# A fused attention and mixer kernel: each side piece gets a place of its own in TensorE's list

## The chip, the core and the metric

The kernel runs on one core of a Trainium2 chip. A core has five engines, each with its own list of instructions that it works through strictly in order: TensorE (PE: matrix products and transposes, with the loads of their stationary operand shown as PEld), VectorE (DVE), ScalarE (ACT), GpSimd (POOL) and SyncE (SP), which here issues all DMA transfers. Engines wait for one another by semaphores. The metric is the device time of one execution in microseconds (us); lower is better. 1% of it, about 6.3 us, is about what a measurement of this kernel can tell from no change.

## The reference, cut to what matters

Four batches (called blocks 0 to 3), 8 heads, 576 positions, head dimension 64, model dimension 512. All weights come as float32 in the low and high words of 64-bit integers and are put together on the chip.

```python
# attention of one batch: a low-resolution softmax attention (means over 4 positions)
s = scale * np.matmul(qq, kk.transpose(0, 1, 3, 2))            # 144 x 144
a = softmax(s);  out_up = np.repeat(np.matmul(a, vv), 4, axis=2)
# plus a local one, |i - j| < 4
scores = np.where(mask, scale * np.matmul(q, k^T), -1e9);  out_local = np.matmul(softmax(scores), v)
# gated convolution: 5 taps along the sequence
gate = 1.0 / (1.0 + np.exp(-gate_pre));  x = (gate * (x @ w_val)) @ w_out
# mixer: over the tokens, then over the channels
h = np.maximum(xt @ w_tok1, 0.0) @ w_tok2;   u = x + h.transpose(0, 2, 1)
h2 = np.maximum(u @ w_ch1, 0.0) @ w_ch2;     return u + h2
```

## The kernel before

**Products.** Every float32 product is split in three: operands are cut into a high and a low part (`hi_lo`, L707), and `mm3` (L273) issues high·high, high·low, low·high. A product row of the trace therefore shows lines L275, L276, L277 in turn. Most have 288 moving columns, half a block's sequence.

**Stages.** `start()` is attention of block 0 in an order written out by hand. Then `first_products` (L889) runs the main stream, per block b: `p1(b)` (L728) with the products p_val (gate times value; y = p_val * gate on VectorE, L747), p_x (output projection, into u_sb), transposes, r_ps (first token product; r_hl on VectorE, L812) and p_h (second token product; u_sb = p_h + u_sb on VectorE, L826, then split to u_hl by ScalarE and GpSimd, L708/L709); then `c1(b)` (L836), the first channel product g_ps in 24 items of 12 matmuls (12 weight tiles f, two sequence halves; 1.6 us each). 12 of the 24 items are issued right after p1(b); the other 12 go between the pieces of p1(b+1) as FILL says (L50). In block 3 all 24 follow at once.

**The second channel product** is done by a scheme with 7 products instead of 8 (two halves of d_ff by two halves of the sequence). It needs, for each of the 6 pairs of weight tiles, four relu results and four sums of them. `c1` makes them: ScalarE writes a relu result into r_sb after each item (L876), after each second weight tile VectorE makes 4 sums of 128x288 (L883), and all 7 slots go to DRAM in `r_dr` (L884). `c2` (L904) loads the slots back (r_back), splits them (g_hl) and multiplies them with ch2 weights (p_o). It runs from 490.24 to 624.41 us of the span. Its last piece adds p_o of two row halves m = 0, 1 into u_back (L927) and stores them (L934).

**Side pieces.** While the main stream runs, `mix` (L990) drops in pieces of other generators: attention of blocks 1 to 3 (`attention(b)`, L329: 26 steps each, four head pairs with low scores sc_d, local scores sc_l, softmax, turns pt_d and pt_l, outputs o_d and o_l into x_f; after each head pair the 5 taps of the convolution, L446 and L449, on VectorE), decoding of the token weights (`w_t1`, `w_t2`), of the ch2 weights (`ch2_new`), and the first two loads of `c2`. Each has a start and an end in microseconds of matmul work of the main stream (T_AT, A_AT, W2_AT, C2_AT), and its steps are spread evenly between. In block 0's c1, the channel weights are decoded too, tile by tile (`ch1_new`: L144, L146, L149, L160 on VectorE, four instructions per 128x256 chunk).

**What sets the order.** TensorE executes in the order in which the program is written. The other four lists are made by a scheduler from dependencies, priorities and its own costs, so moving a piece on TensorE moves rows on all of them. sc_d and sc_l share two PSUM banks: a sc_l product may start only when ScalarE has read (exp, L322) the sc_d that stands in its bank, and the exps wait for VectorE's maxima (mx, L316).

## Time and profile before

| | |
|---|---|
| median of 3 runs | 633.72 us (632.38 to 636.26) |
| profiled execution, whole | 631.51 us |
| its span, first to last instruction | 629.7 us |
| mean granted TensorE clock | 0.963 of full |
| TensorE busy | 585.0 us (93% of the span) |
| VectorE busy | 450.5 us (72%) |
| ScalarE busy | 338.9 us (54%) |
| GpSimd busy | 143.3 us (23%) |

A row of a timeline gives start, duration, engine, line, operation, output<-inputs, shapes, count, and in square brackets how long the engine was idle before it and what released it. A row of a table of windows gives for each engine its busy time and number of instructions, then the granted TensorE clock (1.00 is 2.4 GHz, 0.50 is 1.2 GHz), the share of DMA time used and GB/s. L numbers are lines of the kernel.

### The profile page before, as it was taken

Reading aid. Unit: us, or ns where it says so; the run is one execution under the profiler, and the core shown is the slowest. Engines: PE = TensorE matmul, PEld = TensorE weight load, DVE = VectorE, ACT = ScalarE, POOL = GpSimd, SP = SyncE. Lnnn points to the kernel's source line nnn. Section 1 sums busy time; section 2 is a strip of 40 time slices with the busy share of each in tenths; the row PEclk is TensorE's granted clock in tenths of the full one; section 3 lists DMA queues with packets and bytes.
Section 4 is the critical chain, followed back from the end, with each engine's and each line's share of the span. In section 5 each row is a group of like instructions: output and inputs, shape, how many; then the busy total and the mean of one; then the engine's idle time right before and its main releaser. Section 6 shows DMA issues by size and latency. Waiting matters only on the chain.

```text
span 629.7 us, 13126 instructions
## 1 busy us (share of the span) xinstructions
PE 585.0 (93%) x4975; PEld 536.6 (85%) x4975; DVE 450.5 (72%) x967; ACT 338.9 (54%) x1118; POOL 143.3 (23%) x152
## 2 busy tenths in 40 slices
PE   8885779988979999999999999999999999999996
PEld 3675668778868988998998899998899999999996
DVE  6998976998984568764353578278985677677684
ACT  4985465655556574556635635445352555545542
POOL 1052312372252323515231231310400000000000
PEclk9977789989899999999999999999999999999999
...
GB/s 275 239 176 87 76 115 130 170 148 258 295 175 137 135 149 171 255 328 164 91 121 122 220 293 321 73 195 181 241 313 210 348 360 218 356 214 278 247 4 73
DMA packets 79103, 125.34 MB, mean 199 GB/s; under 512 B 6528, under 2 KB 61824, under 8 KB 79040
## 3 DMA queue, kind: packets, MB, share of 16 engines
...
HBM read 83.99 MB, written 40.50 MB: 198 GB/s over the span
## 4 chain that ended last, share of the span: by engine, by line
PE 59%; DVE 21%; ACT 9%; DMA 5%; POOL 3%; issue 2%; SPq 0%; POOLq 0%; DVEq 0%; ACTq 0%
PE p_o L276 6%; PE g_ps L275 6%; PE p_o L277 6%; PE p_o L275 6%; PE g_ps L276 6%; PE g_ps L277 5%; DVE gate_sb L449 2%; DVE wa L146 2%; PE sc_l L407 2%; ACT e_l L322 2%; PE p_x L275 2%; PE p_val L275 2%; PE p_val L276 2%; PE p_val L277 2%; DVE wa L144 2%
## 5 line engine op out<-in xcount | busy, mean ns | idle before, releaser
L275 PE MATMUL g_ps<-u_hl,w_hl 128*128 128x288 f32 x384 | 118.4, 308 | 0.3 <-DVE u_sb L826 0.3
L276 PE MATMUL g_ps<-u_hl,w_hl 128*128 128x288 f32 x384 | 115.4, 300 | 3.0 <-POOL u_hl L709 2.7
L277 PE MATMUL g_ps<-u_hl,w_hl 128*128 128x288 f32 x384 | 114.5, 298 | 0.0
L708 ACT ACTIVATE g_hl<-r_back 128x384 fp32r<-128x384 f32 x126 | 66.0, 526 | 61.6 <-PE p_o L277 57.1
L709 DVE TENSOR_TENSOR g_hl<-r_back,g_hl 128x384 fp32r<-128x384 f32 x126 | 69.0, 565 | 32.4 <-ACT g_hl L708 31.1
L276 PE MATMUL p_o<-g_hl,ch_w 128*128 128x384 f32 x252 | 84.9, 337 | 1.0 <-DVE g_hl L709 0.6
L277 PE MATMUL p_o<-g_hl,ch_w 128*128 128x384 f32 x252 | 84.7, 336 | 0.0
L275 PE MATMUL p_o<-g_hl,ch_w 128*128 128x384 f32 x252 | 84.5, 335 | 0.0
L276 PEld LDWEIGHTS g_ps<-u_hl,w_hl 128*128 128x128 f32 x384 | 73.5, 191 | 4.3 <-POOL u_hl L709 4.3
L275 PEld LDWEIGHTS g_ps<-u_hl,w_hl 128*128 128x128 f32 x384 | 73.3, 191 | 3.9 <-issue 2.5
L876 ACT ACTIVATE r_sb<-g_ps 128x288 f32<-128x288 f32 x96 | 38.8, 409 | 67.9 <-PE g_ps L277 56.0
L277 PEld LDWEIGHTS g_ps<-u_hl,w_hl 128*128 128x128 f32 x384 | 73.6, 192 | 0.0
L883 DVE TENSOR_TENSOR r_sb<-r_sb 128x288 f32<-128x288 f32 x96 | 48.3, 515 | 29.6 <-ACT r_sb L876 29.0
L276 PEld LDWEIGHTS p_o<-g_hl,ch_w 128*128 128x128 f32 x252 | 47.3, 188 | 2.3 <-DVE g_hl L709 2.3
L449 DVE SCALAR_TENSOR_TENSOR gate_sb<-x_f,cw,gate_sb 128x575 f32<-128x575 f32 (+3 forms) x48 | 47.9, 998 | 0.6
L275 PE MATMUL p_val<-x_hl,val_hi 128*128 128x288 f32 x128 | 41.3, 323 | 7.0 <-DVE x_f L627 5.7
L275 PEld LDWEIGHTS p_o<-g_hl,ch_w 128*128 128x128 f32 x252 | 47.3, 188 | 0.0
L277 PEld LDWEIGHTS p_o<-g_hl,ch_w 128*128 128x128 f32 x252 | 47.3, 188 | 0.0
L275 PE MATMUL p_x<-y_hl,out_hi 128*128 128x288 f32 x128 | 40.7, 318 | 2.0 <-ACT u_sb L760 1.5
L709 POOL TENSOR_TENSOR u_hl<-u_sb,u_hl 128x288 fp32r<-128x288 f32 x32 | 28.3, 898 | 56.1 <-ACT u_hl L708 56.0
L277 PE MATMUL p_x<-y_hl,out_lo 128*128 128x288 f32 x128 | 38.8, 303 | 1.3 <-DVE out_lo L664 1.3
L709 POOL TENSOR_TENSOR x_hl<-x_f,x_hl 128x288 fp32r<-128x288 f32 x28 | 26.3, 953 | 60.1 <-ACT x_hl L708 60.1
(149 smaller groups left out, 1379.0 us busy)
## 6 DMA issues: line engine op xcount, KB each, us to landing
...
r_back<-r_dr SPq DMA_DIRECT2D x21, 1152.0 KB, 6.7
w_hl<-w_dr SPq DMA_DIRECT2D x27, 512.0 KB, 4.9
...
w_dr<-w_hl SPq DMA_DIRECT2D x12, 512.0 KB, 3.8
...
```

The lines of the kernel that those rows point to most:

```text
L144: nc.vector.tensor_scalar(a, x[:, :, 1], 3, 0x3FFFFFF8, ALU.logical_shift_left, ALU.bitwise_and)
L146: nc.vector.scalar_tensor_tensor(out=a, in0=x[:, :, 1], scalar=-0x40000000, in1=a, op0=ALU.bitwise_and, op1=ALU.bitwise_or)
L275: nc.tensor.matmul(out_ap, lhsT=lh, rhs=rh, start=first, stop=False)
L276: nc.tensor.matmul(out_ap, lhsT=lh, rhs=rl, start=False, stop=False)
L277: nc.tensor.matmul(out_ap, lhsT=ll, rhs=rh, start=False, stop=last)
L322: nc.scalar.activation(out=e[:, o, :], in_=p[:, c, :], func=AF.Exp, scale=scale, bias=mx[:, o:o + 1], accum_out=sm[:, o:o + 1])
L407: nc.tensor.matmul(p[r0:r0 + 64, c, :], lhsT=qk[r0:r0 + 64, 0, 3 + o:3 + o + WIN], rhs=qk[r0:r0 + 64, 1, o:o + WIN], start=False, stop=(c ...
L449: nc.vector.scalar_tensor_tensor(out=g[:, sh:], in0=x[:, 0:S - sh], scalar=cw[:, hp, k:k + 1], in1=g[:, sh:], op0=ALU.mult, op1=ALU.add)
L708: nc.scalar.activation(out=hi_ap, in_=src_ap, func=AF.Copy)
L709: lo_eng.tensor_tensor(out=lo_ap, in0=src_ap, in1=hi_ap.bitcast(F32), op=ALU.subtract)
L876: paced[0] = nc.scalar.activation(out=r[:, 2 * (i % 2) + hs], in_=p[:, 0:HS], func=AF.Relu)
L883: nc.vector.tensor_tensor(out=r[:, o], in0=r[:, x], in1=r[:, y], op=op)
```

## The change

1. **Places.** `mix` no longer spreads the steps of a side piece evenly: a table AT names, for each step of each side piece, the position in the main stream (in the same microseconds of matmul work) behind which it is issued. FILL is redistributed too; its sum stays 12, and so do all instructions of TensorE.
2. **First block sums late.** For the first three pairs of weight tiles of block 0 (i < 6) the four sums are not made in `c1`. Only the four relu results are stored (4 slots of 7). A new generator `late_sums` later loads them back in six groups (3 pairs, 2 halves of 144 columns each), makes 4 sums of 128x144 per group, and stores the slots of the sums. The slots are renumbered so that the four raw ones lie together.
3. **Last piece by halves.** In the very last piece of `c2`, all products of row half m = 0 come first, then its add and stores, then those of m = 1. Two of its six g_hl tiles use another pool, since all six now stay live.

```diff
-FILL = {3: 1, 4: 1, 13: 1, 14: 1, 17: 1, 21: 1, 23: 1, 25: 2, 27: 1, 29: 1, 31: 1}
+FILL = {3: 2, 13: 1, 14: 1, 17: 1, 21: 1, 24: 1, 25: 2, 26: 1, 31: 2}
-A_AT = {1: (8, 59), 2: (63, 136), 3: (138, 216)}
-W2_AT = (226, 270), (280, 296)
+AT = {
...
+    "a2": "65.81 65.81 71.42 74.23 77.04 79.85 82.65 85.46 87.59 90.4 93.2 96.01 98.82 102.31 104.81 108.43 "
+        "111.24 114.05 116.86 119.66 124.26 126.42 129.23 132.03 134.84 136.51",
...
+    "late": "142.19 146.08 149.96 153.84 157.71 163.68 167.56",
+}
+    def block_sums(r):
+        for o, x, y, op in ((5, 2, 3, ALU.subtract), (3, 3, 0, ALU.subtract), (4, 5, 0, ALU.add),
+                            (6, 4, 1, ALU.subtract)):
+            nc.vector.tensor_tensor(out=r[:, o], in0=r[:, x], in1=r[:, y], op=op)
+
+    def late_sums():
+        for f in range(NP // 2):
+            for c in (0, HS // 2):
+                r = T(sb, [128, 7, HS // 2], F32, "x2r", NX2, name="r_late")
+                nc.sync.dma_start(out=r[:, 0:4], in_=r_dr[:, f, 0:4, c:c + HS // 2])
+                yield
+                block_sums(r)
+                nc.sync.dma_start(out=r_dr[:, f, 3:7, c:c + HS // 2], in_=r[:, 3:7])
...
                     if i % 2:
-                        for o, x, y, op in ((5, 3, 1, ALU.subtract), (1, 1, 0, ALU.subtract), (4, 5, 0, ALU.add),
-                                            (6, 4, 2, ALU.subtract)):
-                            nc.vector.tensor_tensor(out=r[:, o], in0=r[:, x], in1=r[:, y], op=op)
-                        nc.sync.dma_start(out=r_dr[:, f - NP, :, b * HS:b * HS + HS], in_=r)
+                        late = b == 0 and i < NFT // 2
+                        if not late:
+                            block_sums(r)
+                        n = 4 if late else 7
+                        nc.sync.dma_start(out=r_dr[:, f - NP, 0:n, b * HS:b * HS + HS], in_=r[:, 0:n])
...
-        prods = ((0, 0), (1, 2), (5, 4), (6, 5), (4, 1), (3, 6), (2, 3))
+        prods = ((0, 0), (1, 1), (5, 4), (6, 5), (4, 3), (3, 6), (2, 2))
...
+            ts, ends = [], q == len(pieces) - 1
...
             for k in range(NP):
+                tag, bufs = ("w1", NW1R) if ends and k >= NX2 else ("x2r", NX2)
...
+                for m in range(1 if ends else 2):
+                    product(k, m)
...
+                if ends and m:
+                    for k in range(NP):
+                        product(k, m)
...
-            for j, (g, n, t0, t1) in enumerate(side):
-                want = n if now >= t1 else max(0, int((now - t0) * n / (t1 - t0)))
+            for (g, _), at in zip(side, left):
+                while at and at[0] <= now:
+                    at.pop(0)
+                    next(g, None)
```

**Place one: c1 of block 0, with attention of block 1 beside it.** VectorE before, at the first group of sums (qk_d is a pooled query and key of attention, wa and w_hl are decoded channel weights, x_f is attention's output):

```order
L345 TENSOR_REDUCE qk_d<-qk_sb 128x288
L883 TENSOR_TENSOR r_sb<-r_sb 128x288 x4
L326 RECIPROCAL sm<-sm 128x10
L160 TENSOR_TENSOR w_hl<-wa,w_hl 128x256 x2
L144 TENSOR_SCALAR wa<-w_2034 128x256
L144 TENSOR_SCALAR wa<-w_2036 128x256
L146 SCALAR_TENSOR_TENSOR wa<-w_2034,wa 128x256
```

VectorE after, same place:

```order
L354 TENSOR_REDUCE qk_d<-qk_sb 128x288
L169 TENSOR_TENSOR w_hl<-wa,w_hl 128x256
L335 RECIPROCAL sm<-sm 128x10
L169 TENSOR_TENSOR w_hl<-wa,w_hl 128x256
L153 TENSOR_SCALAR wa<-w_1983 128x256
L153 TENSOR_SCALAR wa<-w_1985 128x256
L155 SCALAR_TENSOR_TENSOR wa<-w_1983,wa 128x256
```

The four sums are gone, here and at two further groups; the decode of the weights follows at once. GpSimd just ahead of this, before (u_hl is the low half of c1's moving operand):

```order
L349 TENSOR_TENSOR vd<-v_sb 72x256
L709 TENSOR_TENSOR u_hl<-u_sb,u_hl 128x288 x4
L327 TENSOR_TENSOR e_l<-e_l,sm 128x640
L709 TENSOR_TENSOR x_hl<-x_f_1059,x_hl 128x288
L348 TENSOR_TENSOR v_sb<-v_sb 72x512
L709 TENSOR_TENSOR u_hl<-u_sb,u_hl 128x288 x4
```

GpSimd after:

```order
L358 TENSOR_TENSOR vd<-v_sb 72x256
L718 TENSOR_TENSOR x_hl<-x_f_1059,x_hl 128x288
L357 TENSOR_TENSOR v_sb<-v_sb 72x512
L336 TENSOR_TENSOR e_l<-e_l,sm 128x640
L718 TENSOR_TENSOR u_hl<-u_sb,u_hl 128x288 x8
```

The three pieces of attention that stood between the two halves of u_hl now stand ahead of both, and the eight run without a break.

**Place two: the end of the first value products of block 1.** TensorE before: the first low scores of block 2's attention (sc_d) come after the first half of p_x; 24 rows ahead of these stand the last p_val:

```order
L276 MATMUL p_x_2412<-y_hl,out_hi 128x288
L277 MATMUL p_x_2412<-y_hl,out_lo 128x288
L359 MATMUL sc_d<-qk_d 72x144 x4
L275 MATMUL g_ps<-u_hl,w_hl 128x288
L276 MATMUL g_ps<-u_hl,w_hl 128x288
```

TensorE after:

```order
L285 MATMUL p_val<-x_hl,val_hi 128x288
L286 MATMUL p_val<-x_hl,val_lo 128x288
L368 MATMUL sc_d<-qk_d 72x144 x4
L284 MATMUL g_ps<-u_hl,w_hl 128x288
L285 MATMUL g_ps<-u_hl,w_hl 128x288
```

sc_d now follows the last p_val, with two c1 items of 12 and the 18 matmuls of p_x between it and the local scores sc_l that share its banks; before it was one item of 12. VectorE before, from the last y of that product to the maxima of sc_d:

```order
L747 TENSOR_TENSOR y_2369<-p_val,gate_sb 128x288
L146 SCALAR_TENSOR_TENSOR wa<-w_2275,wa 128x256
L149 SCALAR_TENSOR_TENSOR wa<-w_2273,wa 128x256
L149 SCALAR_TENSOR_TENSOR wa<-w_2275,wa 128x256
L160 TENSOR_TENSOR w_hl<-wa,w_hl 128x256
L144 TENSOR_SCALAR wa<-w_2470 128x256
L146 SCALAR_TENSOR_TENSOR wa<-w_2470,wa 128x256
L316 TENSOR_REDUCE mx<-sc_d 72x2 x2
```

VectorE after:

```order
L756 TENSOR_TENSOR y_2357<-p_val,gate_sb 128x288
L153 TENSOR_SCALAR wa<-w_2266 128x256
L158 SCALAR_TENSOR_TENSOR wa<-w_2264,wa 128x256
L155 SCALAR_TENSOR_TENSOR wa<-w_2266,wa 128x256
L325 TENSOR_REDUCE mx<-sc_d 72x2
L158 SCALAR_TENSOR_TENSOR wa<-w_2266,wa 128x256
L325 TENSOR_REDUCE mx<-sc_d 72x2
```

Four decode instructions instead of six stand ahead of the second of the two maxima, three ahead of the first.

**Place three: p_h of block 1, where the first late sums stand.** VectorE before:

```order
L449 SCALAR_TENSOR_TENSOR gate_sb<-x_f_2374,cw,gate_sb 128x572
L826 TENSOR_TENSOR u_sb<-p_h,u_sb 128x288 x2
L883 TENSOR_TENSOR r_sb<-r_sb 128x288
L316 TENSOR_REDUCE mx<-sc_d 72x2 x2
L826 TENSOR_TENSOR u_sb<-p_h,u_sb 128x288 x2
L326 RECIPROCAL sm<-sm 72x4
```

VectorE after:

```order
L458 SCALAR_TENSOR_TENSOR gate_sb<-x_f_2362,cw,gate_sb 128x572
L848 TENSOR_TENSOR r_sb<-r_sb 128x288
L835 TENSOR_TENSOR u_sb<-p_h,u_sb 128x288
L848 TENSOR_TENSOR r_sb<-r_sb 128x288
L325 TENSOR_REDUCE mx<-sc_d 72x2 x2
L848 TENSOR_TENSOR r_late<-r_late 128x144 x6
L835 TENSOR_TENSOR u_sb<-p_h,u_sb 128x288
L848 TENSOR_TENSOR r_late<-r_late 128x144
L835 TENSOR_TENSOR u_sb<-p_h,u_sb 128x288
L848 TENSOR_TENSOR r_late<-r_late 128x144
L835 TENSOR_TENSOR u_sb<-p_h,u_sb 128x288
```

Six late sums, and so the landing of their two loads, stand ahead of the second u_sb of the stage. The other 16 late sums stand at three later places: eight ahead of an x_f of block 2's attention, four and four in c1 of block 1.

## Rows read from the trace of the kernel before

**Rows 1.** The page: busy us of each engine, share of the span, instructions

```profile
PE 585.0 (93%) x4975; PEld 536.6 (85%) x4975; DVE 450.5 (72%) x967; ACT 338.9 (54%) x1118; POOL 143.3 (23%) x152
```

**Rows 2.** Windows: stretch, length, busy by engine, clock, DMA share, GB/s

```profile
121.34:173.06 51.72, 46.43 (x433) 41.63 (x433) 46.44 (x94) 29.34 (x108) 22.11 (x21) 0.87 0.74 242
136.00:142.80 6.80, 6.51 (x52) 5.09 (x53) 5.85 (x13) 2.75 (x13) 3.20 (x4) 0.50 0.27 86
156.50:163.30 6.80, 6.80 (x33) 6.12 (x32) 6.80 (x15) 2.71 (x8) 1.19 (x2) 0.50 0.76 248
...
187.20:190.60 3.40, 3.40 (x43) 2.94 (x38) 2.26 (x9) 0.81 (x5) 1.24 (x1) 0.50 0.26 80
...
490.24:624.41 134.17, 133.18 (x758) 131.58 (x756) 98.56 (x198) 69.08 (x136) 0.00 (x0) 1.00 0.71 237
```

**Rows 3.** Timeline of PE: the waits of 0.5 us and more from 121 to 195 us

```profile
135.33 0.40 PE L276 MATMUL g_ps<-u_hl,w_hl 128*128 128x288 f32 x1 [1.80 <-POOL u_hl L709]
...
154.84 0.35 PE L372 MATMUL pt_d<-ident,e_d 72*72 72x72 f32 x3 [1.81 <-DVE x_f L442]
...
173.10 0.40 PE L275 MATMUL p_val<-x_hl,val_hi 128*128 128x288 f32 x1 [0.94 <-DVE y L747]
...
186.63 0.32 PE L401 MATMUL sc_l<-mask,ident 128*128 128x384 bf16 x1 [3.67 <-ACT e_d L322]
...
194.76 0.71 PE L359 MATMUL sc_d<-qk_d 64*72 64x144 f32 x6 [0.60 <-ACT e_l L322]
```

**Rows 4.** Timeline of PE: two waits of block 3's attention

```profile
296.54 0.71 PE L359 MATMUL sc_d<-qk_d 64*72 64x144 f32 x6 [0.72 <-ACT e_l L322]
...
352.84 0.32 PE L401 MATMUL sc_l<-mask,ident 128*128 128x384 bf16 x1 [0.73 <-ACT e_d L322]
```

**Rows 5.** Groups of VectorE from 121.34 to 173.06: busy us, mean ns | idle

```profile
L449 DVE SCALAR_TENSOR_TENSOR gate_sb<-x_f,cw,gate_sb 128x575 f32<-128x575 f32 (+3 forms) x12 | 14.4, 1204 | 0.1
...
L883 DVE TENSOR_TENSOR r_sb<-r_sb 128x288 f32<-128x288 f32 x10 | 4.4, 450 | 0.1
...
L345 DVE TENSOR_REDUCE qk_d<-qk_sb 128x288 f32<-128x1152 f32 x2 | 2.7, 1348 | 2.4 <-DMA qk_sb<-in_qk_dram 2.4
```

**Rows 6.** Timeline of DVE around the low scores of block 2's attention

```profile
178.64 0.44 DVE L747 TENSOR_TENSOR y<-p_val,gate_sb 128x288 f32<-128x288 f32 x1
179.00 0.66 DVE L146 SCALAR_TENSOR_TENSOR wa<-w,wa 128x256 int32<-128x256 int32 x1
...
183.10 0.81 DVE L316 TENSOR_REDUCE mx<-sc_d 72x2 f32<-72x288 f32 x2
```

**Rows 7.** Timeline of DVE at p_h of block 1

```profile
237.98 1.28 DVE L812 SCALAR_TENSOR_TENSOR r_hl<-r_ps,r_hl 128x512 fp32r<-128x512 f32 x2
...
245.16 0.81 DVE L826 TENSOR_TENSOR u_sb<-p_h,u_sb 128x288 f32<-128x288 f32 x2
```

**Rows 8.** Decode groups on DVE, 86 to 100 us, shapes apart

```profile
L149 DVE SCALAR_TENSOR_TENSOR wa<-w,wa 128x256 int32<-128x256 int32 x2 | 0.8, 414 | 0.0
L149 DVE SCALAR_TENSOR_TENSOR wa<-w,wa 128x64 int32<-128x64 int32 x2 | 0.4, 209 | 0.0
```

**Rows 9.** The page: DMA issues, KB each, median us to landing

```profile
r_back<-r_dr SPq DMA_DIRECT2D x21, 1152.0 KB, 6.7
w_hl<-w_dr SPq DMA_DIRECT2D x27, 512.0 KB, 4.9
```

**Rows 10.** Timeline of the end: the last adds and the last four stores

```profile
623.92 1.08 DVE L927 TENSOR_TENSOR u_back<-u_back,p_o 128x384 f32<-128x384 f32 x2 [2.52 <-PE p_o L277]
...
624.51 2.01 SPq L934 DMA_DIRECT2D out_dram<-u_back  x4
```

**Rows 11.** Timelines of POOL and DVE around 133 us

```profile
134.49 3.57 POOL L709 TENSOR_TENSOR u_hl<-u_sb,u_hl 128x288 fp32r<-128x288 f32 x4
...
133.30 4.11 DVE L449 SCALAR_TENSOR_TENSOR gate_sb<-x_f,cw,gate_sb 128x573 f32<-128x573 f32 x1
...
171.87 0.81 DVE L449 SCALAR_TENSOR_TENSOR gate_sb<-x_f,cw,gate_sb 128x572 f32<-128x572 f32 x1
```

More of the change, by code (lines that the diff above doesn't have):

```diff
@@ L38 @@
 NE = 4
-T_AT = (2, 20)
-C2_AT = 262
 NM = 2
@@ L65 @@
 NX2 = 4
-A_AT = {1: (8, 59), 2: (63, 136), 3: (138, 216)}
-W2_AT = (226, 270), (280, 296)
+AT = {
[10 rows of a table added]
+}
+AT = {k: [float(x) for x in v.split()] for k, v in AT.items()}
 NEG = -8.0e9
@@ L950, in c2, with product @@
             acc = [bank(tags[q % len(tags)], "p_o")[:, 0:GW] for _ in range(2)]
+            ts, ends = [], q == len(pieces) - 1
+            def product(k, m):
+                mm3(acc[m], [x[:, m * 128:m * 128 + 128] for x in wt["ch2", k][w]],
+                    [ts[k][:, j] for j in range(2)], k == 0, k == NP - 1)
             for k in range(NP):
-                t = T(sb, [128, 2, GW], F32R, "x2r", NX2, name="g_hl")
+                tag, bufs = ("w1", NW1R) if ends and k >= NX2 else ("x2r", NX2)
+                t = T(sb, [128, 2, GW], F32R, tag, bufs, name="g_hl")
+                ts.append(t)
                 hi_lo(rb[:, k], t[:, 0], t[:, 1], nc.vector)
-                for m in range(2):
-                    mm3(acc[m], [x[:, m * 128:m * 128 + 128] for x in wt["ch2", k][w]],
-                        [t[:, j] for j in range(2)], k == 0, k == NP - 1)
+                for m in range(1 if ends else 2):
+                    product(k, m)
             if i == 0:
@@ L990, in mix @@
     def mix(main_g, side):
-        now, done = 0.0, [0] * len(side)
+        now, left = 0.0, [list(AT[k]) for _, k in side]
         for us in main_g:
             now += us
-            for j, (g, n, t0, t1) in enumerate(side):
-                want = n if now >= t1 else max(0, int((now - t0) * n / (t1 - t0)))
-                while done[j] < want:
-                    done[j] += 1
+            for (g, _), at in zip(side, left):
+                while at and at[0] <= now:
+                    at.pop(0)
                     next(g, None)
-        for g, _, _, _ in side:
+        for g, _ in side:
             run(g)
@@ L1004 @@
     a = [None] + [attention(b) for b in range(1, B)]
-    side = [(chain(w_t1(), w_t2()), 6, *T_AT)]
-    side += [(a[b], NA, *A_AT[b]) for b in range(1, B)]
-    last = c2()
-    w2 = ch2_new()
-    side += [(w2, 8, *W2_AT[0]), (w2, 4, *W2_AT[1]), (last, 1, C2_AT, C2_AT + 1), (last, 1, C2_AT + 8, C2_AT + 9)]
+    side = [(chain(w_t1(), w_t2()), "w")] + [(attention(b), f"a{b}") for b in range(1, B)]
+    side += [(ch2_new(), "ch2"), (c2(), "c2"), (late_sums(), "late")]
     with tc.manual_schedule(engines={mybir.EngineType.PE}):
```

2 lines of the change are left out of this document (1 added, 1 removed), and 7 rows, old and new, of the table AT.

## The prediction

> **What bounds the kernel now.** I read the page first: TensorE is busy 93% of the span, VectorE 72% [rows 1], so the kernel is TensorE's list with holes in it. The list itself does not shrink: the change issues the same matmuls. So the change can only close holes, or open new ones. Next I read the windows. The last stretch, c2, is full: 133.18 of 134.17 us at full clock [rows 2]; nothing is to be had there. The holes are in the stage from 121.34 to 173.06 us (p_h of block 0, then c1 of block 0 with attention of block 1): TensorE 46.43 of 51.72, at a mean clock of 0.87. Two stretches of 6.80 us there are granted only 0.50, that is 1.2 GHz [rows 2]. Third the timeline of TensorE: each of these stretches begins shortly behind the end of a wait (136.00 behind 1.80 us for u_hl that ended at 135.33; 156.50 behind 1.81 us for x_f that ended at 154.84), and behind the 3.67 us that ended at 186.63 there follow another 3.40 us at half clock from 187.20 [rows 2, 3]. A wait is thus paid for twice.
>
> Who is late? In that stage VectorE is busy 46.44 of 51.72 us [rows 2], as much as TensorE: it decodes channel weights, runs the taps of the convolution (14.4 us), and makes 10 of the 12 sums of the first three pairs (4.4 us) [rows 5]. Two of the three waits there, for x_f and for y at 173.10 (0.94 us), name it as the releaser [rows 3].
>
> **The change part by part** (plus is time saved; the sum is made against the profiled execution, 631.5 us with 1.8 outside its span, which is 0.3% below the median of 633.72 us; I subtract from the median).
>
> *Sums of block 0 leave the stage.* Removed there: 10 instructions, 4.4 us at 450 ns [rows 5]. VectorE's list is the slower one in that stage: busy plus waiting it fills it. Low end: its waits (51.72 - 46.44 = 5.3 us) stay as they are and the stage becomes shorter by the 4.4. High end: TensorE needs 46.43 - (6.51 + 6.80) / 2 = 39.8 us with full clock, VectorE 46.44 - 4.4 = 42.0 us without waits; the stage can't be shorter than 42.0, so at most 9.7 are gained. Which? The sums are taken out behind a wait of 2.4 us for a load of qk [rows 5], and a list that comes there earlier waits longer; but the x_f and y that TensorE waited for do come earlier, and with their waits at least one of two half-clock stretches should go (3.4 us each). Nearer to neither end, I take the middle, **+7.0**.
>
> *The steps of attention get new places (place two).* Today sc_l waits 3.67 us for the exps of sc_d, which wait for maxima on VectorE that end at 183.91, 4.9 us behind the y ahead of them [rows 3, 6]: six decode instructions stand between. After, it is four: the six took 178.64 + 0.44 to 183.10, 4.0 us, 0.67 each, so four take 2.7 and the second maximum, at 0.4, ends about 1.3 to 2.7 us earlier (the latter if they run at the 0.42 us of the 128x256 decode [rows 8]); I take 2.2, no more than the wait. TensorE has one more c1 item of 12 (1.6 us) to do meanwhile, and that work would have come later anyway. Low end 0 (VectorE's list as late as today); high end 3.67 + 0.60 at 194.76, and half of the 3.40 at half clock, together 6.0 [rows 2, 3]. Taken: **+2.2**.
>
> *Block 3's attention.* Its steps stand further from what they need; the waits at 296.54 and 352.84, 0.72 and 0.73 [rows 4], are the targets. Low end 0, high end 1.45. Since what is late there is only a fraction of a microsecond, and the steps move by more than that, I take all of it, **+1.5**.
>
> *Late sums.* Added: 24 sums of 128x144, six loads and six stores. A 128x256 of this kind of instruction took 414 ns, a 128x64 took 209 [rows 8], so 144 columns are about 209 + 205 x 80 / 192 = 0.29 us, 7.1 us on VectorE in all, beside TensorE's work nearly everywhere. The exception is place three: six stand ahead of the second u_sb, 1.8 us, and p_h waits for its bank until u_sb is made. Low end 0 (the u_sb row of two starts at 245.16 [rows 7], and p_h may not be waiting), high end 1.8 plus a landing (a rival, below). Taken: **-1.0**. I give the transfers themselves no price: the DMA engines were used to 0.74 even in the busy stage above [rows 2], and c2, which reads the sums, begins only at 490 us; without that room the price would be landings that come later, which is part of D below.
>
> *VectorE's and ScalarE's order in p1 of block 0* shifts by a few decode chunks with the new places of the token weights; TensorE's list there has no row that I can price it by other than single decode instructions, 0.41 us each [rows 8], of which two may come in front of something that TensorE waits for. From 0 to -1.0; taken **-0.5**.
>
> *Last piece by halves.* The last adds run from 623.92 to 625.00 and the last four stores are issued from 624.51 on, over 2.01 us [rows 10]. With the first half's stores out early, only two are left, from about 625.0: at 0.5 us each (a quarter of 2.01) done at 626.0, 0.5 us sooner than 626.5. Against it, m = 0 alone uses up its g_hl tiles in half the time in which both did, and may wait up to that long for the sixth. From -0.3 to +0.5; taken **+0.2**.
>
> Sum: 7.0 + 2.2 + 1.5 - 1.0 - 0.5 + 0.2 = **+9.4 us**: 624.3 by the median.
>
> **The rivals.**
>
> *B, all holes close.* The stage gains its 9.7, place two its 6.0, block 3 its 1.45, the tail 0.5, and the late sums are hidden: 17.7 us, 616. For it: a wait that goes takes its half-clock stretch along [rows 2, 3]. Against: VectorE still has 42.0 us to do in a stage of 42.
>
> *C, the gain is given back.* VectorE comes to its loads earlier and waits for them instead (2.4 us today for one qk [rows 5]), TensorE's waits go elsewhere, and only about 1 us is left: 632.5. For it: TensorE's list has no fewer dependencies than before, and the waits of attention are chains over three engines.
>
> *E, GpSimd's eight u_hl in one run.* While GpSimd ran its four u_hl from 134.49 (3.57 us), one tap on VectorE, begun at 133.30, took 4.11 us; such a tap takes 0.81 when it is alone [rows 11]. After, eight run in a row in the same stage: one more such hold, 4.11 - 0.81 = 3.3 us, off the gain, so 6.1 are left, 627.6. The Trainium skill says in "SBUF — State Buffer", section "Who interferes with whom", that the two engines share a pair of ports under an exclusive lock, so that one of them stands while the other's instruction runs. By that rule, with which the row of 4.11 us agrees, more GpSimd work in one run would hold VectorE longer; the number of u_hl is the same as before, though, and only their bunching is new.
>
> *D, slower: VectorE stands at the head of its list for the late loads.* Its list is strict, and the 24 late sums stand at four places, ahead of u_sb, of x_f, and in c1. The loads need x2r buffers, which come free only when the token product has read them, near the r_hl at 237.98; the first sums stand where u_sb is at about 245.5 [rows 7]. That leaves 7 us for a landing of 4.9 (512 KB) to 6.7 us (1152 KB) [rows 9], plus what stands ahead in SP's list; SP too waits in order, so a load without a buffer holds the weight loads behind it. If at each of four places VectorE stands a landing of 6.7 less about 3 of cover, 3.7, this is 14.8, and two half-clock stretches of 3.4 / 2 more make 18.2: 633.72 - 9.4 + 18.2 = 642.5. It decides (slower by over 1%) from (9.4 + 6.3 - 3.4) / 4 = 3.1 us per place. Against it: 7 us is more than either landing.
>
> **How the numbers follow.** My sum 0.46 (its own range 619 to 630, by the low and high ends: 4.4 in place of 7.0 and 0 in place of 2.2 give 629, 9.7 and 4 give 619.8), B 0.17, C 0.16, E 0.09, D 0.12. Faster by over 1%, below 627.4: 0.39 of my sum, all of B, 0.04 of E, 0.60. Slower, above 640.1: D, 0.12. Within: the rest, 0.28. The range from 614 to 633 takes in my sum, B, E and most of C, and leaves out D and the edges.
>
> **What would show it.** Right: in the stage from r_hl to the first y of block 1 (51.72 us now) less than 46 us, the waits of 1.81 and 0.94 gone and one half-clock stretch less; the wait at sc_l of place two below 1.5 us; the 0.72 and 0.73 gone; late sums at about 0.3 us each without waits for a DMA ahead of them; the last store issued about 0.5 us sooner behind the last matmul. Wrong: VectorE's waits for qk or for weights grown by several us in that stage (C), taps of 4 us or more than one (E), r_late rows with a DMA as releaser and p_h waiting behind (D). The most fragile term is the first: if the stage is bound by the landing of weights rather than by VectorE's instructions, the 7.0 is gone.

## The result

The changed kernel takes 623.37 us (median of 4 runs, 622.50 to 625.18) against 633.05 us of the kernel before on the same chip (629.35 to 636.26): ratio 0.986, 95% interval 0.982 to 0.991. It is faster by 9.7 us in the medians; the forecast was 624.3, a gain of 9.4. The sum was right, but its largest term was far too large and several small ones were too small; they cancelled.

To see where the time went, I cut the span at the first p_val of each block and at the first p_o. Between two such cuts TensorE does the same work before and after, though the order differs. All times in us, from the timelines; "again" is a second profile of the same changed program.

| part of the span | before | after | again | gained | forecast |
|---|---|---|---|---|---|
| to the first p_val | 55.67 | 55.59 | 56.20 | 0.1, -0.5 | 0 |
| block 0: p1 and the first half of c1 | 113.13 | 111.06 | 110.06 | 2.1, 3.1 | 7.0 - 0.5 = 6.5 |
| block 1, with the rest of c1 of block 0 | 112.61 | 110.53 | 110.36 | 2.1, 2.3 | 2.2 - 1.0 = 1.2 |
| block 2, with attention of block 3 | 105.76 | 103.98 | 104.41 | 1.8, 1.4 | 1.5 |
| block 3 | 103.07 | 101.68 | 101.58 | 1.4, 1.5 | 0 |
| c2 up to its last matmul but one | 133.66 | 133.79 | 133.77 | -0.1 | 0 |
| from there to the end | 5.84 | 4.53 | 4.51 | 1.3 | 0.2 |
| span | 629.74 | 621.16 | 620.89 | 8.6, 8.9 | 9.4 |

The page of the changed kernel, busy time by engine (answers to [rows 1]):

```profile
PE 581.0 (94%) x4975; PEld 534.7 (86%) x4975; DVE 450.4 (73%) x979; ACT 337.9 (54%) x1118; POOL 143.8 (23%) x152
```

TensorE has as many instructions as before and 4 us less of busy time; that fits its mean granted clock, which rose from 0.963 to 0.969. Tables of windows, block 0 before and after, and after the stretch from r_hl to the third p_val of block 1 (51.72 us in [rows 2]); columns as in [rows 2]:

```profile
55.67:168.81 113.14, 99.47 (x879) 87.75 (x880) 96.79 (x218) 65.00 (x244) 38.49 (x32) 0.86 0.50 158
```

```profile
123.16:170.00 46.84, 40.38 (x388) 36.95 (x389) 39.87 (x78) 25.19 (x84) 22.47 (x19) 0.96 0.61 202
55.59:166.65 111.06, 95.03 (x879) 84.18 (x880) 94.56 (x208) 67.73 (x248) 37.41 (x32) 0.90 0.47 151
...
132.06:135.47 3.41, 3.41 (x20) 3.35 (x19) 3.10 (x5) 1.31 (x4) 3.10 (x3) 0.50 0.55 175
```

The stretch of the forecast shrank from 51.72 to 46.84 us and its clock rose from 0.87 to 0.96. But r_hl itself now comes 1.8 us later, since some 40 matmuls moved in front of it; over the whole block 0 only 2.1 us are left. Timeline of TensorE, the waits that answer to [rows 3] and [rows 4]:

```profile
128.55 0.40 PE L284 MATMUL p_h<-tok_hl,r_hl 128*128 128x288 f32 x1 [0.98 <-DVE u_sb L835]
...
131.43 0.40 PE L284 MATMUL p_h<-tok_hl,r_hl 128*128 128x288 f32 x1 [1.82 <-DVE u_sb L835]
...
150.20 0.40 PE L286 MATMUL g_ps<-u_hl,w_hl 128*128 128x288 f32 x1 [1.22 <-DVE w_hl L169]
...
159.47 0.41 PE L286 MATMUL g_ps<-u_hl,w_hl 128*128 128x288 f32 x1 [1.48 <-DVE w_hl L169]
...
172.19 0.40 PE L284 MATMUL p_val<-x_hl,val_hi 128*128 128x288 f32 x1 [0.33 <-DVE y L756]
...
182.50 0.32 PE L410 MATMUL sc_l<-mask,ident 128*128 128x384 bf16 x1 [2.04 <-ACT e_d L331]
...
296.46 0.35 PE L368 MATMUL sc_d<-qk_d 64*72 64x144 f32 x2 [0.31 <-ACT e_l L331]
```

The waits of 1.80 for u_hl and 1.81 for x_f are gone, with most of the half clock behind them: of the 13.6 us at 0.50 in [rows 2] one stretch of 3.41 us, from 132.06, is left. In their place stand waits for u_sb inside p_h (2.8 us) and for decoded weights (2.7 us). The wait of 3.67 is 2.04 (in the second profile 0.62, with a wait of 1.26 for y ahead of it and no half clock behind), that of 0.72 is 0.31, that of 0.73 is gone. VectorE, at those places, and the group of the late sums:

```profile
128.42 2.58 DVE L458 SCALAR_TENSOR_TENSOR gate_sb<-x_f,cw,gate_sb 128x575 f32<-128x575 f32 x1
130.93 0.81 DVE L835 TENSOR_TENSOR u_sb<-p_h,u_sb 128x288 f32<-128x288 f32 x2
...
145.76 1.35 DVE L354 TENSOR_REDUCE qk_d<-qk_sb 128x288 f32<-128x1152 f32 x1 [4.66 <-DMA qk_sb<-in_qk_dram]
...
147.49 2.66 DVE L169 TENSOR_TENSOR w_hl<-wa,w_hl 128x256 fp32r<-128x256 f32 x1
```

```profile
L848 DVE TENSOR_TENSOR r_late<-r_late 128x144 f32<-128x144 f32 x24 | 9.7, 433 | 3.2 <-DMA r_late<-r_dr 3.0
```

A tap of 2.58 us has u_sb behind it; before, a tap of 4.11 us [rows 11] had none. VectorE's wait for a load of qk grew from 2.4 [rows 5] to 4.66 us. Behind it one w_hl took 2.66 us where its neighbours take 0.41, while GpSimd worked on two pieces of attention without a break; TensorE's wait of 1.22 us for w_hl ends with it. Such a long single instruction is what the prediction calls a hold; there are more of them below.

### The profile page after: what moved, and what is told of

Read it like the earlier page. It is cut to its first block, busy times and chain, and to the rows that moved or that the text cites. A ratio compares the mean times of both kernels' runs of the same rounds, so it can differ in the third digit from the quotient of the medians.

```text
span 621.2 us, 13166 instructions
## 1 busy us (share of the span) xinstructions
PE 581.0 (94%) x4975; PEld 534.7 (86%) x4975; DVE 450.4 (73%) x979; ACT 337.9 (54%) x1118; POOL 143.8 (23%) x152
## 4 chain that ended last, share of the span: by engine, by line
PE 64%; DVE 19%; ACT 6%; DMA 5%; issue 2%; POOL 2%; SPq 0%; POOLq 0%; DVEq 0%; ACTq 0%
PE g_ps L284 6%; PE g_ps L285 6%; PE g_ps L286 6%; PE p_o L285 6%; PE p_o L286 6%; PE p_o L284 6%; PE p_val L284 3%; PE sc_l L416 2%; PE p_x L284 2%; PE p_val L286 2%; PE p_val L285 2%; DMA qk_sb<-in_qk_dram 2%; DVE gate_sb L458 2%; DVE wa L155 2%; PE p_x L285 2%
## 5 line engine op out<-in xcount | busy, mean ns | idle before, releaser
L284 PE MATMUL g_ps<-u_hl,w_hl 128*128 128x288 f32 x384 | 116.5, 303 | 0.2 <-ACT u_hl L717 0.2
L286 PE MATMUL g_ps<-u_hl,w_hl 128*128 128x288 f32 x384 | 113.4, 295 | 2.7 <-DVE w_hl L169 2.7
L285 PE MATMUL g_ps<-u_hl,w_hl 128*128 128x288 f32 x384 | 113.5, 296 | 0.7 <-POOL u_hl L718 0.7
L718 DVE TENSOR_TENSOR g_hl<-r_back,g_hl 128x384 fp32r<-128x384 f32 x126 | 67.7, 555 | 31.0 <-ACT g_hl L717 29.3
L284 PEld LDWEIGHTS g_ps<-u_hl,w_hl 128*128 128x128 f32 x384 | 72.0, 188 | 3.7 <-issue 2.5
L286 PEld LDWEIGHTS g_ps<-u_hl,w_hl 128*128 128x128 f32 x384 | 72.2, 188 | 3.2 <-DVE w_hl L169 3.2
L285 PEld LDWEIGHTS g_ps<-u_hl,w_hl 128*128 128x128 f32 x384 | 72.2, 188 | 1.3 <-POOL u_hl L718 1.2
L848 DVE TENSOR_TENSOR r_sb<-r_sb 128x288 f32<-128x288 f32 x84 | 39.7, 486 | 29.0 <-ACT r_sb L900 28.5
L284 PE MATMUL p_val<-x_hl,val_hi 128*128 128x288 f32 x128 | 41.3, 322 | 5.9 <-DVE x_f L636 5.6
L458 DVE SCALAR_TENSOR_TENSOR gate_sb<-x_f,cw,gate_sb 128x575 f32<-128x575 f32 (+3 forms) x48 | 45.2, 942 | 0.4
L718 POOL TENSOR_TENSOR u_hl<-u_sb,u_hl 128x288 fp32r<-128x288 f32 x32 | 32.0, 1017 | 53.1 <-ACT u_hl L717 49.3
L285 PE MATMUL p_val<-x_hl,val_hi 128*128 128x288 f32 x128 | 39.7, 310 | 0.0
```

The lines of the kernel that those rows point to most:

```text
L284: nc.tensor.matmul(out_ap, lhsT=lh, rhs=rh, start=first, stop=False)
L285: nc.tensor.matmul(out_ap, lhsT=lh, rhs=rl, start=False, stop=False)
L286: nc.tensor.matmul(out_ap, lhsT=ll, rhs=rh, start=False, stop=last)
L458: nc.vector.scalar_tensor_tensor(out=g[:, sh:], in0=x[:, 0:S - sh], scalar=cw[:, hp, k:k + 1], in1=g[:, sh:], op0=ALU.mult, op1=ALU.add)
L718: lo_eng.tensor_tensor(out=lo_ap, in0=src_ap, in1=hi_ap.bitcast(F32), op=ALU.subtract)
L848: nc.vector.tensor_tensor(out=r[:, o], in0=r[:, x], in1=r[:, y], op=op)
```

## Which part of the change does it: sums, places, or both

**The changed kernel again** (no edit).

> The changed kernel once more, on the chip of the next three. Every theory expects 623.4 us within 1.5, and the four parts of the span (measured between the first value product of one block and that of the next: block 0 111.1, block 1 110.5, block 2 104.0 us, block 3 101.7 up to the second channel product) within 1 us of the first profile; if a part moves by more than 1 us between two executions of the same program, single profiles cannot tell gains of that size.

Measured: 623.17 us (ratio 0.986, 0.982 to 0.990). The table above has its parts: within 1.0 us in block 0 and 0.6 elsewhere. So parts of single profiles are good to about 1 us at best (two profiles of one program below differ by 3.3 us in block 0).

**Late sums alone**, the second part of the change on the kernel before, with the late steps at the numbers of the table:

```diff
...
+                        late = b == 0 and i < NFT // 2
+                        if not late:
+                            block_sums(r)
+                        n = 4 if late else 7
...
+    ls = late_sums()
+    side += [(ls, 1, t, t + 1e-6) for t in (142.19, 146.08, 149.96, 153.84, 157.71, 163.68, 167.56)]
```

> The kernel before, with the first-block sums moved late as the only change (even places, old fillers, old last piece; the late steps at the same numbers of the table). Theory 1 (removed sums are the gain): block 0 shrinks from 113.1 to about 108.7 us, the waits for x_f (1.81) and y (0.94) go, and the time falls from 633 to 629 us. Theory 2 (the places are the gain): block 0 stays at 112 to 113 us and the time at 632 to 634 us.

Measured: 632.32 us (10 runs), ratio 1.001, 0.998 to 1.004: no gain that can be told. And yet block 0 does what theory 1 says: 107.85 us, 5.3 less. It is given back: block 1 takes 115.42 (+2.8), block 2 108.35 (+2.6), block 3 104.11 (+1.0). Timeline of TensorE in this run:

```profile
170.14 0.40 PE L275 MATMUL p_val<-x_hl,val_hi 128*128 128x288 f32 x1 [2.78 <-DVE y L747]
...
183.39 0.48 PE L401 MATMUL sc_l<-mask,ident 128*128 128x384 bf16 x1 [3.39 <-ACT e_d L322]
...
290.48 0.32 PE L401 MATMUL sc_l<-mask,ident 128*128 128x384 bf16 x1 [2.31 <-ACT e_d L322]
```

TensorE arrives sooner and waits at the same places: place two is as long as ever, y is later, and the 0.28 us that sc_l waited at 290.67 before are 2.31. Place two is not the old hole, though. VectorE ahead of it:

```profile
175.74 4.19 DVE L149 SCALAR_TENSOR_TENSOR wa<-w,wa 128x256 int32<-128x256 int32 x1
179.85 0.81 DVE L316 TENSOR_REDUCE mx<-sc_d 72x2 f32<-72x288 f32 x2
```

In the kernel before, six decode instructions stood there; here it is one, but it is held for 4.19 us instead of 0.41, while GpSimd ran seven instructions without a break (173.53 to 179.65). The hold is longer by 3.8 us than the instruction alone, more than the whole wait of 3.39; one profile can't tell whether every execution has it. The wait at 290.48 is made by the late sums themselves. VectorE there:

```profile
286.01 0.65 DVE L839 TENSOR_TENSOR r_late<-r_late 128x144 f32<-128x144 f32 x2 [1.30 <-DMA r_late<-r_dr]
286.58 0.81 DVE L316 TENSOR_REDUCE mx<-sc_d 72x2 f32<-72x288 f32 x2
```

A group stands at the head of VectorE's list, waits 1.30 us for its load, and the maxima of sc_d stand behind it.

**Places and last piece alone**, the changed kernel with all sums made in `c1`, twice:

```diff
-                        late = b == 0 and i < NFT // 2
+                        late = False
-    side += [(ch2_new(), "ch2"), (c2(), "c2"), (late_sums(), "late")]
+    side += [(ch2_new(), "ch2"), (c2(), "c2")]
```

> The changed kernel, but the first-block sums are made in block 0's first channel product as before (12 sums of 128x288, store of seven slots) and there are no late sums; places, fillers and last piece stay changed. Theory 1 (VectorE's list bounds that stage, so the removed sums are the gain): block 0 becomes 4.4 us longer, 115.5 us instead of 111.1, and the time rises to 627 to 628 us, less about 1 us if late sums cost that much in block 1. Theory 2 (the places are the gain, the sums are hidden): block 0 stays within 1 us of 111.1 and the time is 622.5 to 624 us.

> The kernel of the run sums_back once more, for a second profile: its first profiled execution (626.8 us) was the fastest of ten, whose median was 630.9. If its usual time is what the sums cost in block 0, this profile shows block 0 at 114 us or more (112.5 in the first) with block 2 and 3 unchanged at 104.0 and 101.5 us. If the difference lies elsewhere, block 0 stays at 112.5.

Measured: 630.85 us (10 runs, 626.8 to 633.7), ratio 0.998, 0.995 to 1.000. In the two profiles (626.8 and 632.2 us) block 0 took 112.5 and 115.8 us, block 1 112.0 and 113.3; block 2 (104.0) and block 3 (101.5) keep what the places gain there. TensorE's timeline in the second:

```profile
135.89 0.40 PE L284 MATMUL p_h<-tok_hl,r_hl 128*128 128x288 f32 x1 [2.41 <-DVE u_sb L835]
...
156.66 0.40 PE L286 MATMUL g_ps<-u_hl,w_hl 128*128 128x288 f32 x1 [2.83 <-DVE w_hl L169]
...
190.83 0.32 PE L410 MATMUL sc_l<-mask,ident 128*128 128x384 bf16 x1 [3.24 <-ACT e_d L331]
```

So the sums alone gain 0.1 us, the places (with the last piece) alone 1.6 us, and both together 9.3 (medians of this comparison, before 632.4). Neither theory stands alone. Late sums make VectorE free in block 0; waits at y, at place two and beside block 3's attention then take the time back, unless the places close them (for place two, the hold of this one profile has a share); and the places alone leave VectorE full in block 0, so that their own waits (u_sb, w_hl, e_d) stay.

## Place two

The changed kernel with the old order there:

```diff
-FILL = {3: 2, 13: 1, 14: 1, 17: 1, 21: 1, 24: 1, 25: 2, 26: 1, 31: 2}
+FILL = {3: 1, 4: 1, 13: 1, 14: 1, 17: 1, 21: 1, 24: 1, 25: 2, 26: 1, 31: 2}
...
-    "a2": "65.81 65.81 71.42 74.23 77.04 79.85 82.65 85.46 87.59 90.4 93.2 96.01 98.82 102.31 104.81 108.43 "
+    "a2": "65.81 69.00 71.42 74.23 77.04 79.85 82.65 85.46 87.59 90.4 93.2 96.01 98.82 102.31 104.81 108.43 "
```

> The changed kernel, but at place two the old order: one filler, half of p_x, then the low scores of block 2's attention, one filler, then the local scores (FILL back to 3:1, 4:1, and the second number of a2 from 65.81 to 69.00). Theory 1 (the distance between low and local scores is what closed that hole): the wait for the exps grows from 2.04 us (3.67 before the change) back to 3.5 to 4 us, block 1 (from its first value product to that of block 2) from 110.4 to 112.6 us, and the time is 625 to 626 us. Theory 2 (the hole is set by VectorE's list, which comes there earlier or later whatever TensorE does): the wait stays at about 2 us, block 1 within 0.7 of 110.4, the time 623 to 624 us.

Measured: 626.11 us (625.6 to 626.6), ratio 0.991, 0.988 to 0.994: 2.9 us slower than the changed kernel. Block 1 takes 112.07 instead of 110.4. Timelines of this run, TensorE and VectorE:

```profile
185.65 0.32 PE L410 MATMUL sc_l<-mask,ident 128*128 128x384 bf16 x1 [3.75 <-ACT e_d L331]
```

```profile
177.13 0.45 DVE L756 TENSOR_TENSOR y<-p_val,gate_sb 128x288 f32<-128x288 f32 x1
...
182.11 0.81 DVE L325 TENSOR_REDUCE mx<-sc_d 72x2 f32<-72x288 f32 x2
```

and VectorE of the changed kernel:

```profile
175.67 0.45 DVE L756 TENSOR_TENSOR y<-p_val,gate_sb 128x288 f32<-128x288 f32 x1
...
179.34 0.44 DVE L325 TENSOR_REDUCE mx<-sc_d 72x2 f32<-72x288 f32 x1
```

From y to the end of the maxima it is 4.11 us in the changed kernel, 5.79 with the old order, 5.27 before the change [rows 6]; in the second profile of the changed kernel it is 2.63. Theory 1 holds: the place is worth 1.7 us in block 1. The other 1.2 us of the difference lie in block 0, 113.0 against 110 to 111, ahead of the edit, and there VectorE's list is the same as in the changed kernel. TensorE in block 0 of this run:

```profile
138.87 0.48 PE L410 MATMUL sc_l<-mask,ident 128*128 128x384 bf16 x1 [4.29 <-ACT e_d L331]
```

In the changed kernel this wait is 0.85 us. Here a tap of 5.25 us ended at 135.37, ahead of the maxima for that sc_l: a hold that fell on another tap of the same list. So I don't count the 1.2 us for the place.

## Block 3's attention and the late sums

The changed kernel, with a3 at the 26 even places of the kernel before:

```diff
-    "a3": "144.37 147.12 149.87 152.61 155.37 158.11 160.87 163.61 166.35 169.1 171.85 174.6 177.35 180.09 "
...
+    "a3": "141.0001 144.0001 147.0001 150.0001 153.0001 156.0001 159.0001 162.0001 165.0001 168.0001 171.0001 174.0001
...
```

> The changed kernel, but block 3's attention (side piece a3) evenly spaced as before. With the late sums alone on the old kernel (run late_only), a group of late sums waited 1.30 us for its load right ahead of the maxima of sc_d, and TensorE waited 2.31 us at 290.48 (0.28 in the kernel before). Theory 1 (the new places of a3 are what makes the late sums cheap): block 2 grows from 104.0-104.4 to 107 us or more, the time to 626 us or more. Theory 2 (a3's places only close the two waits of 0.72 and 0.73): block 2 grows to 105.5 us, the time to 624.5 to 625 us. Theory 3 (no effect): both stay.

Measured: 628.67 us (10 runs), ratio 0.994, 0.991 to 0.996: 5.4 us slower than the changed kernel. Block 2 takes 108.65 us instead of 104.0 to 104.4, more than in the kernel before (105.76). VectorE and then TensorE in this run:

```profile
282.26 0.65 DVE L847 TENSOR_TENSOR r_late<-r_late 128x144 f32<-128x144 f32 x2 [2.68 <-DMA r_late<-r_dr]
...
283.75 0.81 DVE L324 TENSOR_REDUCE mx<-sc_d 72x2 f32<-72x288 f32 x2
```

```profile
287.67 0.32 PE L409 MATMUL sc_l<-mask,ident 128*128 128x384 bf16 x1 [2.48 <-ACT e_d L330]
```

Theory 1 holds. With even places, the late sums' load is waited for in front of y and of the maxima, at the very next place where TensorE waits for VectorE. In the changed kernel the same waits exist (3.0 us in all, 1.5 at most, in the group shown above), but no maxima stand right behind them. This is the rival D of the prediction, at one place instead of four: the cost of a late sum is not its 0.4 us, it is what stands behind it.

## The last piece

The third part of the change alone, on the kernel before:

```diff
+            ts, ends = [], q == len(pieces) - 1
...
+                for m in range(1 if ends else 2):
+                    product(k, m)
...
+                if ends and m:
+                    for k in range(NP):
+                        product(k, m)
```

> The kernel before with the last piece by halves as the only change. Theory 1 (the halves alone bring the end nearer): from the start of the last matmul to the end of the span 4.2 to 4.6 us instead of 5.8, of which about 0.7 in the issue of the last store and the rest in its landing; the second channel product stays at 133.7 us, so nothing is paid in waits for the sixth tile. Theory 2 (the forecast): 5.3 to 5.6 us, with up to 0.3 us of waiting in front of the last tiles. Before that point nothing should differ from the kernel before by more than one execution differs from another.

Measured: 630.27 us in one execution; from the start of the last matmul but one to the end 4.92 us (5.84 before), c2 133.81. Timelines of this run, VectorE's add of m = 1 and SyncE's last issue of stores (done at 625.51, 1.42 us behind TensorE's last matmul at 624.09):

```profile
624.12 0.56 DVE L927 TENSOR_TENSOR u_back<-u_back,p_o 128x384 f32<-128x384 f32 x1 [2.61 <-PE p_o L277]
```

```profile
619.62 5.89 SPq L934 DMA_DIRECT2D out_dram<-u_back  x5
```

Between the theories. The last store is issued 1.42 to 1.43 us behind TensorE's last matmul in every run with the halves, against 2.11 in the kernel before and 1.86 in late_only. That part, 0.4 to 0.7 us, is the edit's. The rest is landing: the end came 3.7 to 5.2 us behind the last matmul in runs with the halves and 4.4 to 5.3 in the two named without them, so of the 1.3 us in the table no more than about half is shown to be the change. c2 paid nothing: 133.7 to 133.8 us either way.

## Block 0: what ate the gain there

Three runs moved block 1's attention (a1), which lies beside block 0. The changed kernel, in a1_even with all 26 steps of a1 at the even places of the kernel before; in a1_mixed the first 16 steps, then 41.0 and the changed places from the 18th step on; in a1_spread the first 18, then 45.0 and the changed places from the 20th on. The edit of a1_even:

```diff
-    "a1": "9.96 11.75 13.53 15.33 17.12 18.9 20.69 22.48 24.27 26.06 27.85 29.64 30.82 32.61 34.39 36.18 40.24 "
...
+    "a1": "9.9616 11.9232 13.8847 15.8463 17.8078 19.7693 21.7309 23.6924 25.6539 27.6155 29.5770 31.5386 33.5001
...
```

> The changed kernel, but block 1's attention (the side piece a1, beside block 0) is spread evenly again, at the places of the kernel before. In the changed kernel TensorE lost about 4.5 us more than before in p_h of block 0 (waits of 0.37, 0.98 and 1.82 us for r_hl and u_sb and 3.41 us at half clock), with more attention work ahead of r_hl and u_sb in VectorE's list. Theory 1 (the places of a1 cause that loss, and the removed sums help in any case): those waits go, block 0 falls to about 107 us and the time to 619 to 620 us. Theory 2 (the places of a1 pay for themselves in c1): the waits of the kernel before for u_hl (1.80) and x_f (1.81) come back with their half-clock stretches, block 0 is 112 to 114 us and the time 625 to 626 us.

> The changed kernel with block 1's attention evenly spaced (as before) up to its 16th step and at the changed places from then on; the 17th at 41.0. In the run a1_even block 0 took 107.0 us instead of 110 to 111, but block 1 took 112.1 instead of 110.4, with a wait of 2.79 us for y, since the taps ended one c1 item later. Theory 1 (p_h of block 0 wants the old places, the end of c1 the new): block 0 at 107 to 108 us, block 1 at 110.4, the time 619.5 to 620.5 us. Theory 2 (VectorE has so much to do by the end of c1 that what is won early is waited for at its end): the two blocks together stay at 219 to 221 us and the time at 622 to 623 us.

> The changed kernel with block 1's attention evenly spaced (as before) up to its 18th step, which includes the last local scores, and at the changed places from the 19th on. In the run a1_mixed those local scores came one c1 item sooner and TensorE waited 6.02 us for the exps of sc_d; in a1_even the taps came one item later and TensorE waited 2.79 us for y. Theory 1 (both waits come from these places): both go, block 0 at 107 to 108, block 1 at 110.4 to 110.7 us, the time 619.5 to 620.5 us. Theory 2 (they are one wait that moves: VectorE is full until the first y of block 1): blocks 0 and 1 together stay at 219 to 221 us, the time at 622 to 624 us.

| | time, us | ratio | block 0 | block 1 | together |
|---|---|---|---|---|---|
| changed kernel | 623.2 | 0.986 | 111.1, 110.1 | 110.5, 110.4 | 221.6, 220.4 |
| a1_even | 622.71 | 0.986 (0.981 to 0.990) | 107.00 | 112.11 | 219.1 |
| a1_mixed | 626.40 | 0.990 (0.987 to 0.993) | 111.38 | 110.22 | 221.6 |
| a1_spread | 622.87 | 0.984 (0.979 to 0.990) | 112.58 | 109.38 | 222.0 |

In a1_even block 0 falls as theory 1 said, but 1.7 us come back in block 1 and the time stays between the theories; the waits of theory 2 are there only in part (1.05 and 0.60 for u_hl, 0.53 for x_f). In a1_spread theory 2 comes nearer. In a1_mixed the two blocks come near theory 2, and the time is over 3 us longer than either theory said (its profile, 622.5 us, is the fastest of eight executions). In all three, block 0 and block 1 together stay at 219 to 222 us, and none is clearly faster than the changed kernel. The waits mostly move. In a1_even it is y, in a1_mixed sc_l (timelines of TensorE, the first of a1_even, the second of a1_mixed):

```profile
168.64 0.40 PE L283 MATMUL p_val<-x_hl,val_hi 128*128 128x288 f32 x1 [2.79 <-DVE y L755]
```

```profile
137.44 0.48 PE L409 MATMUL sc_l<-mask,ident 128*128 128x384 bf16 x1 [6.02 <-ACT e_d L330]
```

Of these 6.02 us about 3.3 are a hold: a tap of 4.09 us, from 131.47, stands right ahead of the second of the maxima.

Such a hold is what all profiles up to here have in common, one tap of VectorE of 2.6 to 5.3 us near 126 to 133 us, while GpSimd runs its u_hl. The second profile of the changed kernel shows it plainly (VectorE, GpSimd, TensorE):

```profile
128.81 4.10 DVE L458 SCALAR_TENSOR_TENSOR gate_sb<-x_f,cw,gate_sb 128x574 f32<-128x574 f32 x1
132.83 0.45 DVE L835 TENSOR_TENSOR u_sb<-p_h,u_sb 128x288 f32<-128x288 f32 x1
```

```profile
127.48 1.79 POOL L336 TENSOR_TENSOR e_l<-e_l,sm 128x640 f32<-128x640 f32 x1
129.23 4.33 POOL L718 TENSOR_TENSOR u_hl<-u_sb,u_hl 128x288 fp32r<-128x288 f32 x5
```

```profile
133.33 0.40 PE L284 MATMUL p_h<-tok_hl,r_hl 128*128 128x288 f32 x1 [2.41 <-DVE u_sb L835]
```

The tap begins 0.4 us before the u_hl, but GpSimd is at work without a break since 126.23: the tap begins inside its e_l. It ends 0.6 us behind GpSimd's fourth u_hl, in the last of the run; u_sb, and so p_h, waits behind it. In the kernel before it is the same (timeline of GpSimd there): it was at work without a break since 127.66 when the tap of [rows 11] began at 133.30.

```profile
132.00 1.31 POOL L709 TENSOR_TENSOR x_hl<-x_f,x_hl 128x288 fp32r<-128x288 f32 x1
133.27 1.26 POOL L348 TENSOR_TENSOR v_sb<-v_sb 72x512 f32<-72x512 f32 x1
```

If GpSimd's run is the cause, the eight subtractions must leave GpSimd:

```diff
-                hi_lo(uu, us[hs][0][:, c], us[hs][1][:, c], nc.gpsimd)
+                hi_lo(uu, us[hs][0][:, c], us[hs][1][:, c], nc.gpsimd if b else nc.vector)
```

> The changed kernel, but for block 0 the low half of u (u_hl, eight subtractions of 128x288 in p_h) is made by VectorE instead of GpSimd. In every profile so far one tap on VectorE took 2.6 to 5.3 us instead of 0.8 while GpSimd ran its u_hl back to back; in the changed kernel u_sb stands behind that tap, and TensorE's p_h waits 1.8 to 2.4 us for it. Theory 1 (GpSimd's run of u_hl holds VectorE, and that hold is what eats the gain in block 0): no tap over 2 us is left there, the waits of p_h for u_sb shrink to below 0.7 us, block 0 falls from 110-111 to 107-108 us and the time to 620 us. Theory 2 (VectorE's own work is the limit: it gets 8 x 0.45 = 3.6 us more): block 0 stays at 110 us or more, the time at 623 us or more.

Measured: 619.93 us (617.9 to 621.4), ratio 0.980, 0.973 to 0.986: the fastest of all versions, 3.3 us below the changed kernel's 623.2 (the two intervals overlap; the eight executions of the changed kernel lie between 620.5 and 625.2). Block 0 takes 108.03 us, and no single instruction of VectorE between 60 and 310 us takes over 2.0 us. TensorE's waits in p_h, and two groups of VectorE from 120 to 170 us:

```profile
127.39 0.40 PE L284 MATMUL p_h<-tok_hl,r_hl 128*128 128x288 f32 x1 [0.93 <-DVE u_sb L835]
129.13 0.40 PE L284 MATMUL p_h<-tok_hl,r_hl 128*128 128x288 f32 x1 [0.68 <-DVE u_sb L835]
```

```profile
L458 DVE SCALAR_TENSOR_TENSOR gate_sb<-x_f,cw,gate_sb 128x575 f32<-128x575 f32 (+3 forms) x12 | 11.2, 936 | 0.1
L718 DVE TENSOR_TENSOR u_hl<-u_sb,u_hl 128x288 fp32r<-128x288 f32 x8 | 4.3, 583 | 0.0
```

The 12 taps take 11.2 us; in the second profile of the changed kernel the same group took

```profile
L458 DVE SCALAR_TENSOR_TENSOR gate_sb<-x_f,cw,gate_sb 128x575 f32<-128x575 f32 (+3 forms) x12 | 14.4, 1196 | 0.1
```

Theory 1 holds: VectorE pays 4.3 us for the subtractions, gets back 3.2 in taps alone, p_h's longest wait for u_sb falls from 2.41 to 0.93 (not quite the 0.7 expected), and the 3.41 us at half clock that follow that wait in both profiles of the changed kernel are gone: from 95 to 380 us this run's granted clock is 1.00.

Is it the change that makes the hold costly? The same edit on the kernel before:

> The kernel before with block 0's u_hl on VectorE instead of GpSimd as the only change (in the run u_vector the same edit took the changed kernel from 623.2 to 619.9 us and block 0 from 110-111 to 108.0 us). In the kernel before, too, one tap is held for 4.11 us there, but no u_sb stands behind it; GpSimd's last u_hl makes TensorE wait 1.80 us for the first g_ps. Theory 1 (the hold costs only where the change put u_sb behind it): the 1.80 us go, the 3.6 us of new work on VectorE are paid in the full stage behind it, block 0 stays at 112 to 114 us, the time at 631.5 to 633.5 us. Theory 2 (the hold is time lost on VectorE in either kernel): block 0 falls by about 3 us to 110 us, and the time to 629.5 us.

Measured: 632.05 us (10 runs, 627.4 to 638.4), ratio 0.997, 0.994 to 1.001: no difference that can be told. In its profile block 0 fell from 113.1 to 110.6, as theory 2 says, while block 1 rose from 112.6 to 113.6 and block 3 from 103.1 to 104.8. So the time is as theory 1 says and the place as theory 2: once more a gain in block 0 that does not reach the end without the places. Nor did every hold go: one of the subtractions, now on VectorE, took 2.72 us from 128.72 on, while GpSimd worked on attention, and TensorE waited up to 1.89 us for u_hl. Block 3 differs by up to 1.8 us among the four versions without the new places, so with one profile I leave it at that.

## Why the prediction was right, and where not

**The bound and the holes** were read rightly: c2 gave nothing (133.7 before and after), all of the gain came out of waits and the half-clock stretches behind them.

**The sums of block 0, +7.0.** Mis-sized, together with the -0.5 beside it: 2.1 and 3.1 us in block 0 in place of 6.5. The stretch that I named shrank by 4.9, near my low end of 4.4, but 1.8 of that are work moved ahead of it. The removed sums by themselves are worth 5.3 there (late_only), and 6.1 with all of the change but the new places of block 1's attention (a1_even): it is these places that ate the gain there, of which 1.7 come back in block 1. What failed is the step that let the x_f and the y "come earlier" and left the rest of VectorE's list as it was: new rows came in front of r_hl and u_sb, and the held tap moved in front of u_sb. The wait for qk grew by 2.3 us, as I had feared.

**Rival E came true in another shape.** I gave it 0.09 and expected *one more* hold. There was one tap held as before (2.58 and 4.10 us against 4.11), but at a place where TensorE waits behind it; GpSimd's eight u_hl never ran in one go, but five at most. Its price, 3.3 us, is also what u_vector measured (623.2 - 619.9), but made of other parts: TensorE's waits for u_sb fell from 2.8 and 3.0 to 1.6 us, and 3.41 us at half clock went. Nor had I seen that GpSimd's run began ahead of the u_hl. The rule of the Trainium skill that I cited for it ("SBUF — State Buffer", "Who interferes with whom") agrees in kind: no tap over 1.5 us is left in block 0 once GpSimd has no u_hl to do. In size it differs: the page tells of a lock for one instruction, and the rows show a tap that stands through four or five instructions of GpSimd in a row; the measurement decides.

**Place two, +2.2.** Right: 1.7 us in block 1 by ls0_back; in the first profile the wait fell by 1.6 and the half-clock stretch behind it stayed. The maxima came 1.2 us sooner behind y there, just under the lower of the two figures I had, and 2.6 in the second profile. (My upper figure, 2.7, does not follow from its rows: 4.0 less four times 0.42 is 2.3.)

**Block 3's attention, +1.5.** The figure was right (1.8 and 1.4 in block 2) and the reasoning incomplete: with the late sums in the kernel, the same places are worth 4.2 to 4.7 us (a3_even), since they also keep a wait for a load away from the maxima.

**Late sums, -1.0.** Too dear in p_h of block 1, where the loads had landed: TensorE's wait for u_sb rose from 0.45 to 0.68 us only, and one of 1.04 for an sc_l beside it went. Right in kind for their loads, 3.0 us of waiting on VectorE, which the places hide. One late sum took 433 ns on average, not 0.29 us.

**Block 3, 0, and the last piece, +0.2.** Not foreseen: 1.4 us in block 3, which every version with the new places has (101.5 to 102.2 against 103.1 to 104.8 without them); I did not take apart which place, or which of the other moved fillers, does it. The last piece gave 0.4 to 0.7 us of issue and some luck in landing.

So 624.3 came out within 1 us of the result because about 4 us too much in block 0 met about 3.5 us too little in blocks 1 and 3 and at the end. That is luck. Of the signs that I had named, the waits of 1.81 and 0.73 went and those of 0.94 and 0.72 shrank; the stretch did not fall below 46 us (46.84), sc_l at place two not below 1.5 in the first profile (2.04), and late sums did wait for their loads.

What the forecast did not contain at all is that the terms do not add. I had summed them as if each were independent; measured singly they are 0.1 and 1.6 us, and together 9.3.
